# Score products with a pair of heads per row group, one q and one k transfer per tile, and an opening schedule that counts transfers in flight

## The chip, the cores and the metric

The kernel runs on one core of a Trainium2 chip. Its engines are TensorE (PE in the profile; its weight loads are PEld), VectorE (DVE), ScalarE (ACT), GpSimd (POOL) and SyncE (SP), which here only issues transfers. The metric is the device time of one execution in microseconds (us). Three runs of the kernel before gave 946.87, 948.35 and 951.93 us, a median of 948.35 us.

## The reference

Banded attention over 8 batches of 576 positions with 8 heads of 64 features, then a feed-forward layer with a per-channel PReLU. q, k, v and alpha are float32, w_in and w_out float64; the result is float32.

```python
scores = scale * np.matmul(q, k.transpose(0, 1, 3, 2))          # scale = 1/8
mask = (rel >= 0) & (rel < 64)                                  # rel = query - key
scores = np.where(mask, scores, -1000000000.0)
attn = np.exp(scores - np.max(scores, axis=-1, keepdims=True))
attn = attn / (np.sum(attn, axis=-1, keepdims=True) + 1e-09)
x = np.matmul(attn, v)               # then heads side by side: (4608, 512)
h = x @ w_in                         # (512, 2048)
g = np.maximum(h, 0.0) + alpha * np.minimum(h, 0.0)
out = g @ w_out                      # (2048, 512)
```

Each weight is read as two 32-bit words, which the kernel joins into one float32 value.

## The kernel before, in words

The 4608 rows are 36 tiles of 128 rows. A query block of 64 rows sees its own 64 keys and the 64 before, so a tile needs three key blocks of 64. The 13 blocks of the feed-forward layer hold 2 tiles three times, then 3 tiles ten times (`SIZES`). A block passes through 16 cells; cell f is one slice of 128 of the 2048 hidden channels.

**Attention of a tile.** Products of queries and keys (`a_score`, L434 in the profile), masked maximum (`a_least`, L445, DVE), exponential with sum (`a_exp`, L452, ACT), reciprocal (L468), scaling (`a_scale`, L474, POOL), transposition (L491 on PE and a copy, in the opening; L486 on DVE later), product with v (`a_value`, L508), and a split of the result in a high and a low part `xh` and `xl`. A score bank of PSUM holds one of the tile's two query blocks u: its 128 partitions are two heads h of 64 queries, its four column groups the pairs e of heads. The k tile in SBUF has the features of query block u on partitions 64u to 64u+63, with the two key blocks that u sees; the middle key block of a tile stands there twice. It comes in two transfers of 256 KB, and q in four of 64 KB, each of 64 partitions by four runs of 64 numbers.

**Weights.** Each of the 32 half-cells c (even: a slice of w_in, odd: of w_out) is loaded in 512 KB (`fetch`, L327) and converted: bit operations and joins on DVE and ACT, a product (`pr`, L369, POOL), a high part (`hi`, ACT), a low part (`lo`, L384, POOL).

**A cell of a block.** `h` (12 matmuls, L566), slopes on ACT, maximum on DVE, high part `gh` on ACT, low part `gl` on POOL (L595), and per tile three matmuls into the output bank (`o`, L609).

**What sets the order.** Up to the end of block 2 (the opening) the order of all engines is written by `list_schedule`: `opening_graph` gives each step an engine, a duration, its predecessors and the buffers it takes; the step with the highest rank (longest way to the end plus `favour`, a table of numbers) among those ready goes first. Engines then run their steps strictly in that order. From block 3 on, `eighth` and `cell` interleave attention and feed-forward by hand. Transfers are issued from the queue of SP and, for the first two q tiles and alpha, from that of ACT. Eight completion semaphores (DMAHW0 to DMAHW7 in the listings below) are used in turn by all transfers; an issue that takes one still in use by an earlier transfer waits on the issuing engine until that transfer has landed, and everything behind it on this engine waits too. The graph before does not know of these eight lanes.

Of the kernel before, what the change touches and what calls it, by code (L numbers as in the profile page):

```python
# [9 lines left out]
F32 = mybir.dt.float32  # L10
# [26 lines left out]
def opening_graph():  # L37
# [3 lines left out]
    ops = {}  # L41

    def op(name, engine, busy, after=(), take=None, free=(), done=None):
        lag = {"PE": 0.25, "DVE": 0.12, "ACT": 0.13, "POOL": 0.10, "SP": 0.0, "DMA": 1.8}[engine]
        ops[name] = Op(engine, busy, busy + lag if done is None else done, list(after), take, list(free))

    def load(name, service, after=(), take=None, queue="SP"):
        op("i." + name, queue, 0.64, after, take)
        op(name, "DMA", service, ["i." + name])
# [6 lines left out]
    for t in range(EARLY + 1):  # L56
        queue = "ACT" if t < 2 else "SP"
        for u in range(2):
            load(f"k.{t}.{u}", 0.93, [f"s.{t-2}.{x}" for x in range(2)] if t > 1 else [])
            for h in range(2):  # L60
                load(f"q.{t}.{u}.{h}", 0.36, [f"s.{t-2}.{x}" for x in range(2)] if t > 1 else [], queue=queue)
        for u in range(2):
            load(f"v.{t}.{u}", 0.93, [f"av.{t-2}"] if t > 1 else [])
    for c in range(2 * NCELL):
        load(f"raw.{c}", 1.6 if c % 2 else 1.86, take=(f"raw.{c}", ["raw"]))

    for t in attention:
        bank = ["po", "psa"] if t < 2 else ["psa"]
        for u in range(2):
            op(f"s.{t}.{u}", "PE", 0.47, [f"k.{t}.{u}", f"q.{t}.{u}.0", f"q.{t}.{u}.1"]  # L70
               + ([f"s.{t-1}.0", f"s.{t-1}.1"] if t else []) + ([f"av.{t-2}"] if t > 1 else []),
               take=(f"s.{t}.{u}", bank))
# [37 lines left out]
    for n in range(3):  # L110
        pair = [2 * n, 2 * n + 1]
        for f in range(NCELL):
# [9 lines left out]
            for i, t in enumerate(pair):  # L122
                op(f"o.{t}.{f}", "PE", 0.69,
                   [f"gl.{n}.{f}", f"lo.{2*f+1}"] + ([f"o.{t}.{f-1}"] if f else []) + ([f"o.{t-1}.{f}"] if i else []),
                   take=(f"po.{t}", ["psa"] if t == 3 else ["po"]) if f == 0 else None,
                   free=[f"gh.{n}.{f}", f"gl.{n}.{f}"] if i else [])
                if f == last:
                    op(f"ev.{t}", "ACT", 0.55, [f"o.{t}.{f}"], take=(f"ev.{t}", ["raw"]), free=[f"po.{t}"])
                    op(f"i.out.{t}", "SP", 0.64, [f"ev.{t}"])
                    op(f"out.{t}", "DMA", 0.9, [f"i.out.{t}"], free=[f"ev.{t}"])  # L130
# [3 lines left out]
def list_schedule(ops, slots, favour):  # L134
# [24 lines left out]
    while True:  # L159
        for e in ENGINES:  # L160
# [3 lines left out]
            while ready[e]:  # L164
                key = heappop(ready[e])
                n = key[1]
                o, pool = ops[n], None
                if o.take:
                    pool = next((p for p in o.take[1] if left[p]), None)
                    if pool is None:  # L170
                        passed.append(key)
                        continue
                    left[pool] -= 1
                    held[o.take[0]] = pool
                begun[n] = now
                until[e] = now + o.busy
                order.append((n, pool))
# [28 lines left out]
TILE_FAVOUR = [122, 108, 421, -187, -579, -728, -394, -893, 447, -524, -457]  # L206
BLOCK_FAVOUR = [302, 419, -88, 274]
KIND_FAVOUR = dict(
    ad=(75, -133), alpha=(-234, -17), at=(4, 157), av=(-70, 137), ep=(27, 227), ev=(-23, 183),
    ex=(-140, -142), gh=(2, -54), gl=(-152, 142), h=(-163, 317), hi=(-27, -163), k=(-159, 26), la=(95, 31),  # L210
    le=(-217, -229), lo=(-272, -1), mn=(239, -62), mx=(-15, -67), o=(-107, 129), out=(35, -75),
    pr=(34, -352), q=(-94, -45), raw=(-50, 165), rc=(41, 37), s=(-114, 50), sc=(10, 126), sl=(225, 83),
    sm=(126, 51), td=(-235, -80), tu=(-331, 105), tw=(-163, 57), tx=(16, 33), v=(-199, 68), vl=(150, -51),
    xh=(-191, -103), xl=(-89, -85),
# [20 lines left out]
def banded_attention_then_prelu_ffn(  # L235
# [42 lines left out]
    masks = const.tile([P, 2, KW], F32, name="masks")  # L278
    nc.gpsimd.memset(masks, 0.0)

    for h in range(2):
        half = masks[h * W:(h + 1) * W]
        nc.gpsimd.affine_select(out=half, in_=half, compare_op=ALU.is_ge, fill=NEG,
                                base=W, pattern=[[0, 2], [-1, KW]], channel_multiplier=1)
        nc.gpsimd.affine_select(out=half, in_=half, compare_op=ALU.is_gt, fill=NEG,
                                base=0, pattern=[[0, 2], [1, KW]], channel_multiplier=-1)

    nc.gpsimd.memset(masks[:, 1, 0:W], NEG)
# [110 lines left out]
    def k_load(t, u):  # L399
        r = slice(u * D, (u + 1) * D)  # L400
        nc.sync.dma_start(of_tile(t, "k", [P, NP, 2, 2, W])[r].rearrange("d e b h w -> d e (b h w)"),
                          kT[:, :, 2 * t + u:2 * t + u + 2].rearrange("e d b h w -> d e (b h w)"))
# [10 lines left out]
    def load(t):  # L413
        for u in range(2):
            k_load(t, u)
            q_load(t, u, 0)
            q_load(t, u, 1)

# [3 lines left out]
    def a_score(t, halves=(0, 1), from_="psa"):  # L422


        d = st[t]
        q, k = d["q"], d["k"]
        s = d.setdefault("s", {})
        for u in halves:
            s[u] = a_bank(f"s_{t}_{u}", from_)
        for e in range(NP):  # L430
# [93 lines left out]
    def eighth(s):  # L524
# [3 lines left out]
        if k == 0:  # L528
            if t + 1 < NT:
                load(t + 1)  # L530
# [225 lines left out]
```

## Time and profile before

| | us |
|---|---|
| median of 3 runs | 948.35 |
| profiled execution | 949.72 |
| its span, first to last instruction | 948.0 |
| PE busy in the span | 920.7 |
| PE idle from 212 us on, ended by any wait | none |

The profiled execution lies 1.37 us above the median, and 1.7 us of it lie outside the span. PE is busy 97% of the span; DVE, ACT and POOL are busy 46%, 45% and 37%. Idle time of PE is printed with what ended it; the time of an engine that is not waited for costs nothing. A row of the timeline reads: start, duration, engine, line, operation, output<-inputs, shape, count, and in brackets the idle time before it with its releaser. A row of the windows reads: stretch, its length, busy time and count of PE, PEld, DVE, ACT and POOL, the granted TensorE clock, the busy share of the 16 DMA engines, and GB/s.

### The profile page before, as it was taken

The page shows a single profiled execution, that of the slowest core. Times are in us where ns is not written, and L with a number is a line of the kernel's source. Part 1 is how long each engine was busy: PE and PEld are TensorE (multiplying, and loading weights), DVE is VectorE, ACT ScalarE, POOL GpSimd, SP SyncE. Part 2 cuts the span into 40 slices and gives each one's busy share as a digit, 9 for nine tenths or more (in the row PEclk, how much of TensorE's full clock was granted, in tenths as well). Part 3 has the DMA queues.
Part 4 walks back from the last instruction along what each step waited for, and adds up shares of the span by engine and source line. Part 5 has one row for each costly group of instructions (what it writes and reads, how often), then busy time and mean ns, then how long its engine had stood idle before and what let it go on. Part 6 is the DMA issues. An engine that isn't in the chain of part 4 may idle for free.

```text
span 948.0 us, 17231 instructions
## 1 busy us (share of the span) xinstructions
PE 920.7 (97%) x6601; PEld 820.3 (87%) x6601; DVE 437.8 (46%) x1329; ACT 429.6 (45%) x1204; POOL 348.0 (37%) x329
## 2 busy tenths in 40 slices
PE   3989999999999999999999999999999999999998
PEld 2878788888888899888988888888988888898997
DVE  4778885213644444444444443443443444443111
ACT  3777777345434334434434344443443443432322
POOL 3679897232323322322332222233222223322221
PEclk9989999999999999999999999999999999999999
DMA  9997553123233323323323323223323332100000
GB/s 220 215 208 186 165 164 102 44 47 79 57 59 87 57 56 90 57 56 89 57 56 90 56 57 90 57 56 57 89 56 57 87 59 56 57 1 1 34 1 34
DMA packets 94385, 74.52 MB, mean 79 GB/s; under 512 B 42576, under 2 KB 87648, under 8 KB 94304
## 3 DMA queue, kind: packets, MB, share of 16 engines
q1 hardware_dynamic: 92096, 72.90, 35.0%
q8 instruction: 52, 0.85, 0.4%
q10 hardware_dynamic: 2208, 0.53, 0.4%
q14 instruction: 29, 0.24, 0.1%
HBM read 63.97 MB, written 9.44 MB: 77 GB/s over the span
## 4 chain that ended last, share of the span: by engine, by line
PE 87%; DMA 5%; POOL 2%; DVE 2%; issue 1%; ACT 1%; ACTq 0%; SPq 0%; DVEq 0%; POOLq 0%
PE h L566 40%; PE o L609 39%; PE s L434 4%; PE av L508 4%; DMA raw<-w_in 2%; DMA k<-kT 1%; DMA v<-vN 1%; POOL gl L595 1%; DMA q<-qT 1%; POOL val L369 1%; DMA raw<-w_out 1%; DVE two L336 0%; PE t L491 0%; POOL wout_l L384 0%; DVE man L346 0%
## 5 line engine op out<-in xcount | busy, mean ns | idle before, releaser
L595 POOL TENSOR_TENSOR gl<-g,gh 128x384 fp32r<-128x384 f32 (+1 forms) x208 | 197.1, 947 | 556.8 <-ACT gh L588 551.3
L581 DVE SCALAR_TENSOR_TENSOR g<-h,s_sb,g 128x384 f32<-128x384 f32 (+1 forms) x208 | 121.8, 586 | 337.1 <-ACT g L575 336.4
L575 ACT ACTIVATE g<-h,sa_sb 128x384 f32<-128x384 f32 (+1 forms) x208 | 115.5, 556 | 264.4 <-PE h L566 261.5
L609 PE MATMUL o<-wout_h,gl 128*128 128x512 f32 x576 | 228.5, 397 | 1.1 <-POOL gl L595 0.9
L609 PE MATMUL o<-wout_l,gh 128*128 128x512 f32 x576 | 227.3, 395 | 0.0
L609 PE MATMUL o<-wout_h,gh 128*128 128x512 f32 x576 | 224.7, 390 | 0.0
L566 PE MATMUL h<-xh,win_h 128*128 128x384 f32 (+1 forms) x832 | 175.2, 333 | 2.3 <-DVE g L581 2.3
L566 PE MATMUL h<-xl,win_h 128*128 128x384 f32 (+1 forms) x832 | 170.0, 326 | 0.0
L566 PE MATMUL h<-xh,win_l 128*128 128x384 f32 (+1 forms) x832 | 169.1, 325 | 0.0
L566 PEld LDWEIGHTS h<-xh,win_h 128*128 128x128 f32 x832 | 142.4, 190 | 21.5 <-DVE g L581 4.2
L588 ACT CAST gh<-g 128x384 fp32r<-128x384 f32 (+1 forms) x208 | 101.6, 489 | 129.2 <-DVE g L581 117.7
L486 DVE STREAM_TRANSPOSE pt<-w 32x256 f32<-32x256 f32 x324 | 141.2, 436 | 5.5
L566 PEld LDWEIGHTS h<-xl,win_h 128*128 128x128 f32 x832 | 143.6, 190 | 0.1
L566 PEld LDWEIGHTS h<-xh,win_l 128*128 128x128 f32 x832 | 140.9, 190 | 0.0
L609 PEld LDWEIGHTS o<-wout_h,gh 128*128 128x128 f32 x576 | 108.4, 188 | 24.3
L609 PEld LDWEIGHTS o<-wout_h,gl 128*128 128x128 f32 x576 | 108.5, 188 | 18.8 <-POOL gl L595 2.6
L452 ACT ACTIVATE w<-w,nm 128x128 f32<-128x128 f32 x288 | 113.1, 396 | 21.0 <-DVE nm L445 20.9
L609 PEld LDWEIGHTS o<-wout_l,gh 128*128 128x128 f32 x576 | 108.7, 189 | 13.5
L474 POOL TENSOR_TENSOR w<-w,rc 128x1024 f32<-128x1024 f32 (+1 forms) x45 | 70.0, 1555 | 15.6 <-DVE rc L468 15.5
L445 DVE CUSTOM_DVE_ANT_0 w<-s,masks 128x128 f32<-128x128 f32 x288 | 70.8, 283 | 4.9 <-PE s L434 4.5
L520 DVE TENSOR_TENSOR xl<-av,xh 128x512 fp32r<-128x512 f32 x36 | 24.8, 690 | 103.0 <-ACT xh L515 103.0
L434 PE MATMUL s<-k,q 64*64 64x128 f32 x1152 | 53.8, 292 | 15.3 <-DMA q<-qT 11.9
(46 smaller groups left out, 527.7 us busy)
## 6 DMA issues: line engine op xcount, KB each, us to landing
k<-kT SPq DMA_DIRECT2D x72, 256.0 KB, 5.0
v<-vN SPq DMA_DIRECT2D x72, 256.0 KB, 4.3
out<-os SPq DMA_DIRECT2D x36, 256.0 KB, 2.3
q<-qT SPq DMA_DIRECT2D x136, 64.0 KB, 4.7
raw<-w_in SPq DMA_DIRECT2D x16, 512.0 KB, 4.8
raw<-w_out SPq DMA_DIRECT2D x16, 512.0 KB, 6.2
q<-qT ACTq DMA_DIRECT2D x8, 64.0 KB, 6.2
alpha_rows<-alpha ACTq DMA_DIRECT2D x1, 8.0 KB, 4.0
```

What stands on the lines that cost most here:

```text
L434: nc.tensor.matmul(s[u][out_, e], q[r, e, h, :], k[r, e, :, h, :], start=True, stop=True)
L445: nc.vector.tensor_tensor_reduce(out=d["w"][:, g, :], in0=d["s"][u][:, e], in1=mask, op0=ALU.add, op1=ALU.min, scale=-SCALE, scalar=3.0e38 ...
L452: nc.scalar.activation(w, w, AF.Exp, scale=-1.0, bias=d["nm"][:, g:g + 1], accum_out=d["sm"][:, g:g + 1])
L474: nc.gpsimd.tensor_tensor(out=w, in0=w, in1=rc.unsqueeze(2).broadcast_to(list(w.shape)), op=ALU.mult)
L486: nc.vector.transpose(pt[ks, :, r], w[r, :, ks])
L508: nc.tensor.matmul(av[r, e, u * W:(u + 1) * W], v[:, e, u, r], pt[:, u * NP + e, h * W:(h + 1) * W], start=True, stop=True)
L566: nc.tensor.matmul(ph[:, :nt], wt[:, c, fs], xt[:, c, xs], start=(k == 0), stop=(k == 3 * NP - 1))
L575: nc.scalar.activation(g, ph[:, :nt], AF.Copy, scale=sa_sb[:, f:f + 1])
L581: nc.vector.scalar_tensor_tensor(out=g, in0=ph[:, :nt], scalar=s_sb[:, f:f + 1], in1=g, op0=ALU.mult, op1=ALU.max)
L588: nc.scalar.copy(gh, gs[n, f])
L595: nc.gpsimd.tensor_tensor(out=gl, in0=g, in1=gh.bitcast(F32), op=ALU.subtract)
L609: nc.tensor.matmul(po[t], gt[:, ts], wt[:, f, :], start=(f == 0 and k == 0), stop=(f == NF - 1 and k == 2))
```

## The change

**Layout of the scores.** A row group of 64 partitions now holds one head x of a pair instead of one query block. A score bank holds head x of each pair; its partitions are the two query blocks u, its columns the pairs (a, h). So q and k need only one copy of each number: k is 128 partitions by two runs of 384 numbers (three key blocks, 384 KB), q 128 partitions by two runs of 256 numbers (256 KB), one transfer each. Masks get a third variant, and `a_value` reads its weights under the new index. Counts and shapes of the matmuls, of the DVE and of the ACT steps stay as they are.

**Order of the score products.** In tiles 0 to 2 (`WHOLE`) the products of both banks are one step of the opening, alternating between the row groups; in tiles 3 to 8 of the opening each bank is still a step of its own. From block 3 on both banks alternate, as before.

**The schedule.** `lane=8` is a buffer that every transfer takes at its issue and frees when it lands. Durations in the graph are changed (loads, scores), and both tables of `favour` hold other numbers.

```diff
+WHOLE = (0, 1, 2)
-SLOTS = dict(ph=2, psa=3, po=3, raw=3, exp=2, val=2, g=2, gh=3, gl=3)
+SLOTS = dict(ph=2, psa=3, po=3, raw=3, exp=2, val=2, g=2, gh=3, gl=3, lane=8)
...
+    def load(name, service, after=(), take=(), queue="SP"):
+        op("i." + name, queue, 0.64, after, [take] * bool(take) + [("lane " + name, ["lane"])])
+        op(name, "DMA", service, ["i." + name], free=["lane " + name])
...
-        queue = "ACT" if t < 2 else "SP"
+        done = [f"s.{t-2}.0", f"s.{t-2}.1"] if t > 1 else []
+        load(f"q.{t}", 1.05, done, queue="ACT" if t == 0 else "SP")
+        load(f"k.{t}", 1.6, done)
...
-        load(f"raw.{c}", 1.6 if c % 2 else 1.86, take=(f"raw.{c}", ["raw"]))
+        load(f"raw.{c}", 2.0 if c % 2 else 2.2, take=(f"raw.{c}", ["raw"]))
...
+        if t in WHOLE:
+            op(f"s.{t}.0", "PE", 0.94, score, take=[(f"s.{t}.0", bank), (f"s.{t}.1", bank)])
+            op(f"s.{t}.1", "PE", 0.0, [f"s.{t}.0"], done=0.0)
...
-TILE_FAVOUR = [122, 108, 421, -187, -579, -728, -394, -893, 447, -524, -457]
+TILE_FAVOUR = [305, -52, 78, 372, -192, -315, -70, -391, 34, -311, -259]
...
-    def k_load(t, u):
-        r = slice(u * D, (u + 1) * D)
-        nc.sync.dma_start(of_tile(t, "k", [P, NP, 2, 2, W])[r].rearrange("d e b h w -> d e (b h w)"),
-                          kT[:, :, 2 * t + u:2 * t + u + 2].rearrange("e d b h w -> d e (b h w)"))
-
-    def q_load(t, u, h, queue=None):
-        r = slice(u * D, (u + 1) * D)
-        (queue or nc.sync).dma_start(of_tile(t, "q", [P, NP, 2, W])[r, :, h, :],
-                                     qT[:, :, t, h, u * W:(u + 1) * W].rearrange("e d q -> d e q"))
+    def q_load(t, queue=None):
+        (queue or nc.sync).dma_start(of_tile(t, "q", [P, 2, 2 * P]),
+                                     qT[:, :, t].rearrange("(a x) d h p -> (x d) a (h p)", x=2))
+
+    def k_load(t):
+        nc.sync.dma_start(of_tile(t, "k", [P, 2, 6 * W]),
+                          kT[:, :, 2 * t:2 * t + 3].rearrange("(a x) d b h w -> (x d) a (b h w)", x=2))
...
-        for e in range(NP):
+        for x, from_ in zip(halves, banks):
+            s[x] = a_bank(f"s_{t}_{x}", from_)
+        for a in range(2):
             for h in range(2):
-                for u in halves:
-                    r, out_ = slice(u * D, (u + 1) * D), slice(h * W, (h + 1) * W)
-                    nc.tensor.matmul(s[u][out_, e], q[r, e, h, :], k[r, e, :, h, :],
-                                     start=True, stop=True)
+                for u in range(2):
+                    for x in halves:
+                        r, us = slice(x * D, (x + 1) * D), slice(u * W, (u + 1) * W)
+                        nc.tensor.matmul(s[x][us, 2 * a + h], q[r, a, h, us], k[r, a, u:u + 2, h, :],
+                                         start=True, stop=True)
```

Three places show how the order moves. First, the transfers at the start, each with the semaphores its issue waits for: SP before (raw is a half-cell of weights).

```order
L327 DMA raw_117<-w_in 128x4x256
L327 DMA raw_120<-w_out 128x1024
L327 DMA raw_123<-w_in 128x4x256
L401 DMA k_126<-kT 64x4x256 [waits DMAHW1_49]
L401 DMA k_126<-kT 64x4x256 [waits DMAHW4_49]
L401 DMA k_132<-kT 64x4x256 [waits DMAHW6_49]
L401 DMA k_132<-kT 64x4x256 [waits DMAHW7_49]
L410 DMA v_139<-vN 64x4x256 [waits DMAHW0_49]
```

And SP now:

```order
L410 DMA k_118<-kT 128x2x384
L414 DMA v_121<-vN 64x4x256 x2
L406 DMA q_124<-qT 128x2x256
L410 DMA k_126<-kT 128x2x384
L333 DMA raw_128<-w_in 128x4x256
L333 DMA raw_130<-w_out 128x1024 [waits DMAHW0_49]
L333 DMA raw_150<-w_in 128x4x256 [waits DMAHW1_49]
L414 DMA v_152<-vN 64x4x256 [waits DMAHW2_49]
L406 DMA q_167<-qT 128x2x256 [waits DMAHW3_49,PE_49]
L410 DMA k_169<-kT 128x2x384 [waits DMAHW4_49]
```

The three weight loads stood ahead of the first k and now stand behind q and k of two tiles. ACT's queue before held eight q transfers of 64 KB and alpha, of which four waited for a lane; it now holds q of tile 0 and alpha, and neither waits.

Second, PE up to the first cell `h_0`. Before (s_0 and s_1 of one tile are its banks, t its transpositions):

```order
L434 MATMUL s_0_165<-k_126,q_115 64x128 x8
L434 MATMUL s_1_185<-k_126,q_115 64x128 x8
L434 MATMUL s_0_208<-k_132,q_128 64x128 x8
L491 MATMUL t_0_240<-ident,w_177 128x128 x4
...
L491 MATMUL t_0_315<-ident,w_221 128x128 x4
L434 MATMUL s_0_340<-k_235,q_200 64x128 x8
L434 MATMUL s_1_356<-k_235,q_200 64x128 x8
L491 MATMUL t_1_369<-ident,w_221 128x128 x4
L508 MATMUL av_396<-pt_110,v_146 64x64 x16
L434 MATMUL s_0_424<-k_307,q_260 64x128 x8
L491 MATMUL t_0_438<-ident,w_351 128x128 x4
L566 MATMUL h_0_449<-xh,win_h 128x256 x4
```

Now (in tiles 0 to 2 the rows of s_0 and s_1 alternate eight times):

```order
L433 MATMUL s_0_132<-k_118,q_116 64x128
L433 MATMUL s_1_133<-k_118,q_116 64x128
...
L651 MATMUL alpha_t<-ident,alpha_rows 128x16
L433 MATMUL s_0_186<-k_126,q_124 64x128
...
L490 MATMUL t_0_282<-ident,w_208 128x128 x4
L433 MATMUL s_0_306<-k_169,q_167 64x128
...
L490 MATMUL t_1_357<-ident,w_208 128x128 x4
L507 MATMUL av_371<-pt_111,v_152 64x64 x16
L433 MATMUL s_0_392<-k_227,q_213 64x128 x8
L433 MATMUL s_1_408<-k_227,q_213 64x128 x8
L565 MATMUL h_0_432<-xh,win_h 128x256 x4
```

Both banks of tile 3 now stand ahead of `h_0`, and the first transposition of tile 2 behind it.

Third, POOL around the second scaling of tile 1 (w_221 before, w_208 now), on which the transposition t_1 of that tile waits. Before:

```order
L474 TENSOR_TENSOR w_221<-w_221,rc_224 128x512
L369 TENSOR_TENSOR val_304<-val_304,exp_163 128x512
L369 TENSOR_TENSOR val_313<-val_313,exp_197 128x512
L474 TENSOR_TENSOR w_221<-w_221,rc_224 128x512
L384 TENSOR_TENSOR wout_l<-val_304,wout_h 128x512
```

Now:

```order
L473 TENSOR_TENSOR w_208<-w_208,rc_211 128x512
L375 TENSOR_TENSOR val_292<-val_292,exp_280 128x512
L375 TENSOR_TENSOR val_301<-val_301,exp_294 128x512
L390 TENSOR_TENSOR win_l<-val_292,win_h 128x4x128
L473 TENSOR_TENSOR w_208<-w_208,rc_211 128x512
```

The first half-cell's low part is now made between the two scalings; before, half-cell 0 was done ahead of both.

More of the change, by code (lines that the diff above doesn't have):

```diff
@@ L41, in opening_graph, with op @@
     ops = {}
-    def op(name, engine, busy, after=(), take=None, free=(), done=None):
+    def op(name, engine, busy, after=(), take=(), free=(), done=None):
         lag = {"PE": 0.25, "DVE": 0.12, "ACT": 0.13, "POOL": 0.10, "SP": 0.0, "DMA": 1.8}[engine]
[L45 to L49, printed above, removed]
+        ops[name] = Op(engine, busy, busy + lag if done is None else done, list(after), [take] if take and isinstance(take[0], str) else list(take), list(free))
+    def load(name, service, after=(), take=(), queue="SP"):
+        op("i." + name, queue, 0.64, after, [take] * bool(take) + [("lane " + name, ["lane"])])
+        op(name, "DMA", service, ["i." + name], free=["lane " + name])
     attention = range(EARLY)
@@ L128, in opening_graph @@
                     op(f"ev.{t}", "ACT", 0.55, [f"o.{t}.{f}"], take=(f"ev.{t}", ["raw"]), free=[f"po.{t}"])
-                    op(f"i.out.{t}", "SP", 0.64, [f"ev.{t}"])
-                    op(f"out.{t}", "DMA", 0.9, [f"i.out.{t}"], free=[f"ev.{t}"])
+                    load(f"out.{t}", 0.9, [f"ev.{t}"])
+                    ops[f"out.{t}"].free.append(f"ev.{t}")
     return ops
@@ L166, in list_schedule @@
                 n = key[1]
[L167 to L174, printed above, removed]
+                o, got = ops[n], []
+                for key_, pools in o.take:
+                    p = next((p for p in pools if left[p] > got.count(p)), None)
+                    got.append(p)
+                if None in got:
+                    passed.append(key)
+                    continue
+                for (key_, _), p in zip(o.take, got):
+                    left[p] -= 1
+                    held[key_] = p
                 begun[n] = now
                 until[e] = now + o.busy
-                order.append((n, pool))
+                order.append((n, got))
                 heappush(ends, (now + o.busy, 0, n))
@@ new lines, in scores @@
+    def scores(t, u, banks):
+        if t not in WHOLE:
+            a_score(t, (u,), banks)
+        elif u == 0:
+            a_score(t, (0, 1), banks)
+    steps = {
+        "at": lambda got: alpha_turned(), "ad": lambda got: signs(),
+        "i.alpha": lambda got: nc.scalar.dma_start(alpha_rows, alpha.rearrange("(f p) -> f p", p=P)),
+        "i.k": lambda got, t: k_load(t), "i.q": lambda got, t: q_load(t, nc.scalar if t == 0 else None),
+        "i.v": lambda got, t, u: v_load(t, u),
+        "i.raw": lambda got, c: fetch(c),
+        "i.out": lambda got, t: m_store(t),
+        "s": lambda got, t, u: scores(t, u, got),
+        "le": lambda got, t, g: a_least(t, g),
+        "ex": lambda got, t, g: a_exp(t, g),
+        "sm": lambda got, t, u: a_sum(t, (u,)),
+        "rc": lambda got, t, u: a_inverse(t, (u,)),
+        "sc": lambda got, t, u: a_scale(t, (u,)),
+        "tu": lambda got, t, u: a_turn(t, u, got[0]),
+        "td": lambda got, t, u: a_turned(t, u),
+        "av": lambda got, t: a_value(t, got[0]),
+        "xh": lambda got, t: a_xh(t), "xl": lambda got, t: a_xl(t),
+        "tw": lambda got, c: mask_exponent(c), "tx": lambda got, c: exponent(c),
+        "mn": lambda got, c: mask_mantissa(c), "mx": lambda got, c: signed_mantissa(c),
+        "ep": lambda got, c: sign(c), "vl": lambda got, c: join(c),
+        "pr": lambda got, c: product(c), "hi": lambda got, c: high_part(c),
+        "lo": lambda got, c: low_part(c),
+        "h": lambda got, n, f: m_hidden(n, f), "sl": lambda got, n, f: m_slopes(n, f),
+        "la": lambda got, n, f: m_larger(n, f), "gh": lambda got, n, f: m_high(n, f),
+        "gl": lambda got, n, f: m_low(n, f),
+        "o": lambda got, t, f: m_add(t // 2, f, t % 2), "ev": lambda got, t: m_evict(t),
```

90 lines of the change are left out of this document (28 added, 62 removed).

## The prediction

> **What bounds the kernel now.** I read the page first, then what PE waited for, then windows over the span.
>
> ```profile
> PE 920.7 (97%) x6601; PEld 820.3 (87%) x6601; DVE 437.8 (46%) x1329; ACT 429.6 (45%) x1204; POOL 348.0 (37%) x329
> PE   3989999999999999999999999999999999999998
> ```
>
> PE is busy almost throughout; the holes are in the first slices. The waits of PE up to 212 us:
>
> ```profile
> PE s L434 <- DMA q<-qT: 11.9, 1, 11.9
> PE t L491 <- POOL w L474: 3.2, 1, 3.2
> PE s L434 <- DMA k<-kT: 2.9, 2, 2.4
> PE h L566 <- DVE g L581: 2.3, 2, 2.0
> PE av L508 <- DVE pt L496: 1.2, 2, 0.8
> PE o L609 <- POOL gl L595: 0.9, 1, 0.9
> PE s L434 <- DVE val L363: 0.6, 1, 0.6
> ```
>
> They add up to 23.0 us of idle time; behind 212 us the same view has no row. So the 736 us from block 3 on are PE work back to back, and what an engine or a transfer gains there is hidden. The change keeps the matmuls there: same counts, same shapes, and banks alternating between row groups before and after. It can move the time only through the opening, and what PE loses or gains there goes to the end one for one.
>
> ```profile
> 2.00:12.00 10.00, 0.12 (x2) 0.16 (x4) 1.98 (x3) 1.55 (x2) 1.35 (x5) 1.00 1.11 248
> 12.00:67.00 55.00, 46.29 (x433) 39.11 (x434) 40.83 (x148) 38.97 (x131) 34.54 (x31) 0.95 1.08 216
> 67.00:160.00 93.00, 90.53 (x648) 78.33 (x648) 73.62 (x168) 69.52 (x175) 84.14 (x80) 0.98 0.60 158
> 212.00:948.00 736.00, 731.81 (x5100) 657.04 (x5099) 310.04 (x971) 296.28 (x838) 211.88 (x187) 1.00 0.27 58
> ```
>
> Three stages in the opening. To 67 us the DMA engines are full (share 1.08) at 216 GB/s; the other engines wait in turns. From 67 to 160 us POOL is the busiest beside PE (84 of 93 us, mostly weights). Then PE alone. In the first stage PE also runs at half rate for long:
>
> ```profile
> 11.88 1.97 PE L434 MATMUL s<-k,q 64*64 64x128 f32 x16 [11.88 <-DMA q<-qT]
> 14.34 2.90 PE L434 MATMUL s<-k,q 64*64 64x128 f32 x32 [0.49 <-DMA k<-kT]
> 20.40 1.12 PE L491 MATMUL t<-ident,w 128*128 128x128 f32 x4 [3.16 <-POOL w L474]
> 25.46 1.76 PE L508 MATMUL av<-pt,v 128*64 128x64 f32 x28 [0.37 <-DVE pt L496]
> 28.20 2.89 PE L434 MATMUL s<-k,q 64*64 64x128 f32 x32
> 33.36 1.76 PE L508 MATMUL av<-pt,v 128*64 128x64 f32 x28 [0.81 <-DVE pt L496]
> 37.72 1.20 PE L566 MATMUL h<-xh,win_h 128*128 128x256 f32 x4
> 40.43 0.63 PE L491 MATMUL t<-ident,w 128*128 128x128 f32 x4
> 61.64 1.97 PE L434 MATMUL s<-k,q 64*64 64x128 f32 x16 [0.57 <-DVE val L363]
> 228.51 1.10 PE L434 MATMUL s<-k,q 64*64 64x128 f32 x32
> ```
>
> Four transpositions take 1.12 us at 20.40 and 0.63 at 40.43: up to about 40 us the clock is half, although the profile's clock column still prints 1.00 there. It falls twice more, where the column shows it:
>
> ```profile
> 60.00:70.00 10.00, 9.43 (x64) 8.45 (x65) 7.58 (x26) 6.60 (x21) 7.04 (x8) 0.66 1.06 221
> 110.00:120.00 10.00, 7.95 (x40) 6.85 (x40) 7.18 (x13) 5.93 (x12) 7.52 (x9) 0.83 0.47 159
> ```
>
> At 0.66 and 0.83 of full speed for 10 us, 3.4 and 1.7 us are lost, each behind a gap of 2 to 3 us.
>
> The Trainium skill, "TensorE: Matmul & The Clock Gate", part 1 on the HAM clock gate, says that the clock halves after an idle window of about 3.4 us and opens after about as much sustained work. The trace disagrees both ways: a gap of 2.0 us was followed by half rate, and the 7.1 us without a gap from 33.36 to 40.43 were needed to open it. By the rule, short gaps would cost themselves only, and the last term below would have 5.1 us less to win; as no place of the trace bears it out, it gets no chance of its own.
>
> **The change, part by part.**
>
> *The first wait, -6.3 us.* Before, three weight loads stand ahead of k, and ACT stands in its own queue until a lane is free.
>
> ```profile
> 0.80 0.44 SPq L327 DMA_DIRECT2D raw<-w_in  x1
> 5.12 6.49 SPq L401 DMA_DIRECT2D k<-kT  x4
> 5.13 0.69 DVE L346 TENSOR_SCALAR man<-raw 128x512 int32<-128x512 int32 x1 [4.14 <-DMA raw<-w_in]
> 10.44 1.28 ACT L341 ACT_TABLE_LOAD   x1 [10.44 <-DMA q<-qT]
> 4.00:6.00 2.00, 0.00 (x0) 0.00 (x0) 0.87 (x2) 0.00 (x0) 0.00 (x0) 1.00 1.05 314
> ```
>
> The first weight load, 524 KB at the head of SP's queue beside q on ACT's, was usable at 5.13. Now q (262 KB) heads one queue and k (393 KB) the other. 655 KB at 248 to 314 GB/s, from about 2 us on, are there at 4.1 to 4.6, and half a microsecond for completion and overlap with v behind k gives about 5.1; I take 5.6. Bounds: 4.8, and 8.3 if all 1.8 MB issued first come at once. PE starts at 5.6 instead of 11.88.
>
> *Score products, -2.4 us of work ahead of the first cell.* In the table above, 16 matmuls of one bank cost 1.97 us at half rate, and 32 alternating ones 1.10 at full rate, so about 2.2 at half rate (no row shows it). Tiles 0 to 2 cost 1.97 + 2.90 + 1.97 + 2.89 = 9.7 before (32 of them from 14.34 take 2.90) and 3 x 2.2 = 6.6 now: -3.1. Against it, bank 1 of tile 3 moves ahead of the first cell (+0.9, from 1.97 to 2.89) and a transposition behind it (-1.1), which come back later with the other sign; with small remainders of the alpha and value steps I take -2.4. Bounds: 0, if a whole tile at half rate costs 2.9 and the gaps absorb it, and -4.
>
> *Gaps ahead of the first cell, +4.7 us.* Before, they are 0.49, 3.16, 0.37 and 0.81, together 4.8. Now by the order listed: tile 1's q and k are the last of 1.84 MB, at 270 GB/s (between the windows' 248 and 314) at about 9.3; the scores of tile 0 end at 7.8, so 1.5. Then t_0 of tile 0: before, the first maximum ran at 16.00 and the transposition at 20.40, 4.4 us later; now the first maximum is at 7.9, and the alpha steps (0.8 us of DVE) stand between: 13.1 against an end of tile 1's scores at 11.5, so 1.6. Small ones 0.3. Tile 2's k ends 4.3 MB, at 270 GB/s about 18.5, no gap. The large one is t_1 of tile 1. It waits for the second scaling on POOL, now queued behind two products and a low part, and in PE's order the scores of tiles 2 and 3 don't both stand ahead of it.
>
> ```profile
> 16.00 0.28 DVE L445 CUSTOM_DVE_ANT_0 w<-s,masks 128x128 f32<-128x128 f32 x1
> 26.35 2.51 POOL L369 TENSOR_TENSOR val<-val,exp 128x512 f32<-128x512 f32 x2 [0.52 <-DVE val L363]
> 28.82 1.03 POOL L474 TENSOR_TENSOR w<-w,rc 128x512 f32<-128x512 f32 x1
> 31.05 1.27 POOL L384 TENSOR_TENSOR win_l<-val,win_h 128x512 fp32r<-128x512 f32 x1
> 13.62 0.68 DVE L363 SCALAR_TENSOR_TENSOR val<-raw,man 128x512 f32<-128x512 uint32 x1
> ```
>
> DVE's steps of that stretch at 0.6 each put the first product's input at about 21.5 and the second's at 23.3; then 1.28 (POOL), 1.27 and 1.03 end the scaling at 26.9, t_1 at 27.0, where PE has been free since 21.8: 5.2. A copy before the values of tile 1 adds 0.9. Sum 9.5, so +4.7. Bounds: 0 (DVE's estimate is 5 us late) and +9.
>
> The three terms put the first cell at about 33.7 instead of 37.72: -4.0.
>
> *The rest of the opening, -4.0 us.* Before, PE loses 0.9, 2.4, 0.6, 2.3 in gaps and 3.4 and 1.7 in clock behind 38 us: 11.3. What was late there was data:
>
> ```profile
> 30.21 8.82 DMA k<-kT
> 39.05 8.60 DMA v<-vN
> 47.71 10.02 DMA raw<-w_in
> q1 hardware_dynamic: 2280, 3.39, 55.8%
> q1 hardware_dynamic: 36976, 24.91, 30.3%
> ```
>
> The chain of waits runs through three transfers from 30 to 57.7 us. What they cost comes from the two last rows, which are 80 to 100 us (mostly weights: 2280 packets and 3.39 MB in 55.8% of 16 engines for 20 us, 78 ns and 1487 bytes each) and 300 to 700 us (tiles: 36976 packets, 24.91 MB, 52 ns and 674 bytes). A straight line through both is an estimate of 31 ns a packet and 0.032 ns a byte. A tile's q, k and v before are 1024 packets of 256 bytes and 1024 of 1 KB: 105 us of one engine, 6.6 us of all 16. Now 256 and 512 of 1 KB and 256 of 1.5 KB: 69, or 4.3 us. About six tiles loaded from 12 to 67 us thus free some 13 us of DMA time. POOL and DVE get work earlier but have as much of it, 35 and 41 us from 12 to 67 us. In the order listed POOL also holds `gl` of the first cell ahead of four steps that are ready, some 4 us. So I take a third of the 11.3 us. Bounds: -11.3, and +6 if a new gap of 2.4 us with 3.4 us of clock is added.
>
> The Trainium skill, "DMA: Bandwidth & Descriptors", rules for kernel authors, asks for one transfer of 128 partitions instead of two of 64, since both share the same engines. By that, the halves cost no more than one transfer and only the repeated key block (131 KB of 1.31 MB a tile) would be saved, 0.6 us a tile at 216 GB/s; the rest of this term would have to come from the packets.
>
> *Later.* A tile's 2.2 us of DMA time less, its four issues less on SP and the third mask are worth nothing behind 212 us: DMA share is 0.27 there and no wait of PE ends. If that cover were gone the transfers would gain 36 x 2.2 us at most, but PE's back-to-back work doesn't allow it.
>
> Sum: -6.3 - 2.4 + 4.7 - 4.0 = -8.0. The profiled execution, 949.72 (span 948.0 and 1.7 outside), would become 941.7. It stands 1.37 above the median, so against the median I forecast 940.3.
>
> **The rivals.**
>
> *The lead is given back (944 to 950).* PE starts 6 us earlier, but the weights come later: the first weight load was usable at 5.13 and is now the sixth transfer, at about 11. If POOL's queue of conversions sets PE's pace at 45 to 60 us (by the steps above, the low part of half-cell 4 ends at about 47.5 against 45.65 + 1.31 before), the lead becomes a gap at h or o of the first cells, and only the shorter score work and about 1 us are left: about -3, 945.5. For it: POOL's stretch from 67 us is 90% busy. Against: in the same time PE can work on tile 3 and block 1, which the order has earlier.
>
> *Slower (953 to 958).* The mechanism is the clock behind POOL's gap. If t_1 of tile 1 waits beyond 30 us (POOL's products wait for ACT, which is behind tile 1's exponentials), the first cell is no earlier than before, and tile 3, h and o then come in short bursts with gaps of over 2 us, each paying 2.4 us and 3.4 of clock as at 60 us. From two such gaps more than before it decides: +11.6, less the 6.3 of the start, +5.3, about 953.5.
>
> *All of it (930 to 934).* The DMA time freed carries through: no gap at 60 and 115 us, both drops of the clock gone. Then the last term is -11.3 and the sum -15.3: 933. For it, the chain of waits; against, POOL's 84 of 93 us.
>
> *The transfers are no cheaper.* If a packet costs by its bytes, DMA saves 10% of a tile; the start is won all the same, the last term falls to about -1: 943.5, inside the forecast's range.
>
> **How the numbers follow.** The forecast (-5 to -12) has 0.55, with the cheap-transfer case in it; the lead given back 0.22; slower 0.09; all of it 0.14. A measurement of this kernel tells 0.5%, 4.7 us, from no change. Faster by more: the forecast and all of it, 0.69, less 0.02 for its edge, 0.67. Within 0.5%: 0.23. Slower: 0.10. The likeliest case alone reaches from 936 to 943.5; the range that leaves out some 2 in 10 goes from 931.5 to 947.5.
>
> **What would show it.** The first score matmul at 5 to 6.5 us; scores of tile 0 in about 2.2 us; a gap of some 5 us at PE's t, released by POOL, between 20 and 28 us; the first h at 32 to 35 us; DMA below full share before 67 us, by a tile's cheaper loads; no wait of PE for k or q later than 20 us; nothing changed from block 3 on (some 736 us). A first h later than 37 us, or more than two waits over 2 us of PE between 40 and 120 us, would make the forecast wrong; so would any change of the length of the late stage.

## The result, and the profile after

The changed kernel takes 934.48 us (median of 4 runs, 934.10 to 934.98), the kernel before 950.14 (4 runs, 946.87 to 952.83). The ratio is 0.9837, with a 95% interval of 0.9801 to 0.9873: 1.6% faster. The profiled execution took 934.54, with a span of 932.8 us against 948.0, so 15.2 us less. The forecast was 940.3; what came is nearest to the case listed as "all of it" (930 to 934), 0.5 us above its upper edge.

Windows over the span of the changed kernel (columns as before):

```profile
2.00:12.00 10.00, 3.93 (x65) 3.49 (x65) 2.54 (x22) 4.22 (x17) 2.50 (x7) 1.00 1.07 289
12.00:67.00 55.00, 46.53 (x432) 37.97 (x426) 48.08 (x148) 44.55 (x139) 41.31 (x39) 1.00 0.81 223
67.00:160.00 93.00, 92.71 (x691) 81.60 (x690) 68.67 (x156) 68.38 (x167) 80.98 (x79) 1.00 0.47 146
197.00:932.80 735.80, 732.10 (x5102) 657.23 (x5100) 310.35 (x971) 296.55 (x839) 211.90 (x187) 1.00 0.19 53
```

The late stage is the same length, 735.8 us against 736.0, and begins 15 us earlier. From 12 to 67 us the DMA share fell from 1.08 to 0.81 while the bytes per second rose a little, and DVE and POOL were busier in the same stretch: 48.1 and 41.3 us against 40.8 and 34.5. What PE waited for up to 197 us:

```profile
PE s L433 <- DMA q<-qT: 6.1, 1, 6.1
PE t L490 <- POOL w L473: 3.4, 3, 1.6
PE s L433 <- DVE nm L444: 2.0, 1, 2.0
PE s L433 <- DVE val L369: 1.9, 2, 1.2
PE o L608 <- POOL gl L594: 1.2, 2, 1.0
PE t L490 <- DVE pt L495: 0.9, 1, 0.9
PE t L490 <- DVE val L369: 0.5, 1, 0.5
PE av L507 <- DVE pt L495: 0.3, 2, 0.2
PE h L565 <- DVE g L580: 0.3, 1, 0.3
```

Together 16.6 us, against 23.0. All but 0.6 of the 6.4 us are the first wait; the later ones are as long in sum (10.5 against 11.1) but shorter one by one. And the timeline of PE:

```profile
6.06 1.98 PE L433 MATMUL s<-k,q 64*64 64x128 f32 x32 [6.06 <-DMA q<-qT]
10.27 2.10 PE L433 MATMUL s<-k,q 64*64 64x128 f32 x32 [2.01 <-DVE nm L444]
21.43 0.69 PE L433 MATMUL s<-k,q 64*64 64x128 f32 x2 [0.72 <-DVE val L369]
23.28 1.98 PE L433 MATMUL s<-k,q 64*64 64x128 f32 x30 [1.16 <-DVE val L369]
26.86 1.12 PE L490 MATMUL t<-ident,w 128*128 128x128 f32 x4 [1.61 <-POOL w L473]
32.86 0.74 PE L565 MATMUL h<-xh,win_h 128*128 128x256 f32 x4
38.11 0.50 PE L608 MATMUL o<-wout_h,gl 128*128 128x512 f32 x1 [1.02 <-POOL gl L594]
```

The first `h` runs at full rate (0.74 us for four; 1.20 before), so the clock opens at about 32.6 instead of 40.4, and the clock column prints 1.00 from there to the end of the opening: neither drop of before comes back. An account of the 15.2 us, which is an estimate in that half rate counts as half of the busy time under it: before, 23.8 us of work up to 40.4 cost 11.9, and the two drops 5.1, together 17.0; now 18.0 us of work up to 32.6 cost 9.0. That is 8.0 us from the clock, 5.8 from the first wait (11.88 to 6.06), 0.6 from the later waits, and the remainder, about 1, goes to the shorter score work by subtraction alone.

### The profile page after: what moved, and what is told of

The parts are those of the page before. It is cut to its first block, busy times and chain, and to the rows that moved or that the text cites. A ratio compares the mean times of both kernels' runs of the same rounds, so it can differ in the third digit from the quotient of the medians.

```text
span 932.8 us, 17053 instructions
## 1 busy us (share of the span) xinstructions
PE 912.3 (98%) x6601; PEld 812.3 (87%) x6601; DVE 438.0 (47%) x1329; ACT 430.5 (46%) x1204; POOL 348.1 (37%) x330
## 4 chain that ended last, share of the span: by engine, by line
PE 94%; DVE 2%; POOL 2%; ACT 1%; DMA 1%; issue 0%; POOLq 0%; DVEq 0%
PE h L565 43%; PE o L608 42%; PE s L433 4%; PE av L507 4%; PE t L490 1%; ACT w L451 1%; POOL val L375 1%; DMA q<-qT 1%; POOL w L473 0%; POOL gl L594 0%; POOL wout_l L390 0%; POOL win_l L390 0%; DVE exp L363 0%; DVE val L369 0%; DVE two L342 0%
## 5 line engine op out<-in xcount | busy, mean ns | idle before, releaser
L433 PEld LDWEIGHTS s<-k,q 64*64 64x64 f32 x1152 | 39.4, 142 | 24.0 <-PE o L608 9.6
```

What stands on the lines that cost most here:

```text
L433: nc.tensor.matmul(s[x][us, 2 * a + h], q[r, a, h, us], k[r, a, u:u + 2, h, :], start=True, stop=True)
```

## The experiments

Each but the last was timed beside the kernel before, whose medians there were 947.9 to 948.7. Differences below are against the changed kernel's 934.5 or against the neighbour named.

**New layout and transfers, order of before.**

```diff
-        "i.k": lambda pool, t, u: k_load(t, u),
-        "i.q": lambda pool, t, u, h: q_load(t, u, h, nc.scalar if t < 2 else None),
+        "i.k": lambda pool, t, u: k_load(t) if u == 0 else None,
+        "i.q": lambda pool, t, u, h: q_load(t, nc.scalar if t < 2 else None) if u + h == 0 else None,
...
-        "s": lambda pool, t, u: a_score(t, (u,), pool),
+        "s": lambda pool, t, u: a_score(t, (u,), (pool,)),
```

This is the kernel before with `k_load`, `q_load`, `a_score`, `a_value` and the masks of the change; its graph, slots and tables stay. k and q of a tile go out whole at the place of their first part.

> The kernel before, with the new layout of q, k and scores and its single transfers of q and k per tile, but the opening written in the order of before: old graph, no lanes, old tables, scores bank by bank, three weight loads first. Theory A (the transfers' DMA time is what the opening won): the DMA-bound stretch up to 67 us shortens, the gap at 60 us and both drops of the clock go, the first score still waits for the weight loads (9 to 11 us); 938 to 942, so two thirds or more of the 15 us. Theory B (the planned order is what won): the order of before stalls at other places as it did, 945 to 950.

Measured: 934.53 (933.10 to 936.03), ratio 0.9862 (0.9839 to 0.9886). Theory A said 938 to 942 and theory B 945 to 950; both are too high, B is out. The order of before, fed by the new transfers, is as fast as the newly planned one. Its waits, windows and timeline:

```profile
PE s L428 <- DMA k<-kT: 10.3, 1, 10.3
PE t L485 <- POOL w L468: 2.7, 2, 2.3
PE av L502 <- DVE pt L490: 1.8, 2, 1.6
```

```profile
12.00:67.00 55.00, 48.96 (x502) 41.87 (x497) 46.38 (x170) 47.31 (x162) 43.29 (x41) 0.97 0.81 230
```

```profile
10.27 3.81 PE L428 MATMUL s<-k,q 64*64 64x128 f32 x48 [10.27 <-DMA k<-kT]
31.00 1.20 PE L560 MATMUL h<-xh,win_h 128*128 128x256 f32 x4
```

It starts PE 4 us later than the changed kernel, since its weight loads go first, and still has the first `h` 2 us earlier. Its conversions begin earlier: DVE's first step on a weight comes at 5.5 us, and at 14.5 in the changed kernel. The DMA share is the same 0.81. The clock column reads 0.97 because of one piece of 3.4 us at half rate from about 30.4 on, which the second row above shows (1.20 us for four `h`). It follows a wait of 1.62 us:

```profile
28.52 0.92 PE L502 MATMUL av<-pt,v 128*64 128x64 f32 x24 [1.62 <-DVE pt L490]
```

This kernel has the new layout, the new transfers and the freed queue of ACT together. So it shows that the gain does not need the new plan, and not yet which part of the transfers brings it.

**q in runs of 256 bytes, one transfer.**

```diff
-        (queue or nc.sync).dma_start(of_tile(t, "q", [P, 2, 2 * P]),
-                                     qT[:, :, t].rearrange("(a x) d h p -> (x d) a (h p)", x=2))
+        (queue or nc.sync).dma_start(of_tile(t, "q", [P, 2, 2 * P]).rearrange("p a (g w) -> p (a g) w", g=4),
+                                     qT[:, :, :, :, t].rearrange("a g x d w -> (x d) (a g) w"))
```

> The changed kernel with one thing undone: q lies in memory so that one transfer of 256 KB consists of 1024 runs of 256 bytes instead of 256 runs of 1 KB. Same order, same number of transfers, same bytes. Theory A (price by packets, 31 ns each from the two rows in the prediction): 768 packets more are 24 us of one engine, 1.5 us of all 16 per tile, DMA near full up to 50 us again; 936 to 940, with the first score 0.5 to 1 us later. Rival (price by bytes): 934 to 935 and a first score at 6.1.

Measured: 934.29 (933.57 to 935.68), first score at 5.8. No time is lost, as the rival said, though the packets have a price. The DMA groups from 300 to 700 us give the price of the runs, first this kernel, then the changed one:

```profile
q1 hardware_dynamic: 32451, 23.28, 24.1%
```

```profile
q1 hardware_dynamic: 19764, 23.09, 21.0%
```

12687 packets more for nearly the same bytes take 3.1% of 16 engines for 400 us, 198 us: 16 ns each, half of the 31 that I worked out. DMA share from 12 to 67 us rises from 0.81 to 0.87, still below full, and behind the first two tiles' scores no wait of PE ends with a transfer.

**q and k in two transfers of 64 partitions.**

```diff
-        nc.sync.dma_start(d, kT[:, :, 2*t:2*t+3].rearrange("(a x) d b h w -> (x d) a (b h w)", x=2))
+        for x in range(2):
+            nc.sync.dma_start(d[x * D:(x + 1) * D], kT[x::2, :, 2*t:2*t+3].rearrange("a d b h w -> d a (b h w)"))
```

q is split in the same way.

> The changed kernel with q and k of a tile each in two transfers of 64 partitions instead of one of 128: same packets, same bytes, same order, two issues more per tile and lanes used up faster than the plan counts. If the number of transfers matters (issue time, 0.4 to 0.6 us each on SP, and lanes): waits of SP for lanes in the first 60 us and 936 to 939. If only packets and bytes matter: 934 to 935.

Measured: 937.38 (936.92 to 938.90), ratio 0.9895 (0.9875 to 0.9915): 2.9 us more. The packets of a tile are the same (this window holds 0.9 MB more), yet the share from 300 to 700 us rises:

```profile
q1 hardware_dynamic: 21200, 23.99, 24.8%
```

```profile
12.00:67.00 55.00, 46.01 (x439) 37.64 (x432) 45.80 (x144) 43.71 (x139) 39.38 (x37) 0.88 0.95 225
```

From 21.0% with 23.09 MB to 24.8% with 23.99 MB; the bytes alone would be 21.8. So halves cost DMA time of their own, about as much for each MB as the short runs of q did (1.03% for each MB in both runs, 0.91% in the changed kernel), and from 12 to 67 us the engines are near full again. Whether the 2.9 us come from that or from the additional issues is not separated: up to 70 us, SP's waits that end with a transfer add up to 4.0 us here and to 1.7 in the changed kernel. The Trainium skill, "DMA: Bandwidth & Descriptors", rules for kernel authors, says that two halves share the same engines and that one transfer of 128 partitions is to be used. The advice holds here; the reading that halves cost no more than the whole, on which the prediction weighed it, does not.

**Scores of tiles 0 to 2 bank by bank.**

```diff
-            a_score(t, (0, 1), banks)
+            a_score(t, (0,), banks[:1])
+            a_score(t, (1,), banks[1:])
```

> The changed kernel with the score products of tiles 0 to 2 written bank after bank, in the same places of PE's order, instead of alternating between the row groups. If they set the pace: 32 of them take 2.9 instead of 2.0 us at half rate, two of the three on the chain that ends last, so the first h 1.5 to 2.5 us later and 936 to 937. Rival: they end in the gaps in front of t, 934.5.

Measured: 935.94 (934.74 to 936.72), 1.5 us above the changed kernel, at the edge of what the runs tell apart. Tile 0's scores take 2.89 us instead of 1.98 and the first `h` comes at 33.82 instead of 32.86, which supports the first reading with about half its size for `h`. Tile 1 also shows what its scores wait for; the view of the changed kernel names DVE (`nm`), and here it is k:

```profile
10.13 2.89 PE L433 MATMUL s<-k,q 64*64 64x128 f32 x32 [0.79 <-DMA k<-kT]
```

**Lanes not counted in the plan.**

```diff
-SLOTS = dict(ph=2, psa=3, po=3, raw=3, exp=2, val=2, g=2, gh=3, gl=3, lane=8)
+SLOTS = dict(ph=2, psa=3, po=3, raw=3, exp=2, val=2, g=2, gh=3, gl=3, lane=99)
```

> The changed kernel, with 99 lanes in the planner's graph, so that it plans as if any number of transfers could be in flight; tables and everything else as in the change. If counting the lanes matters, the order has issues that wait on SP for a lane with others behind them, and the time is 937 to 942. Rival: with so few transfers eight lanes hardly bind, 934 to 936.

Measured: 934.80 (934.22 to 935.57). The rival holds: with one transfer each for q and k, counting lanes is worth nothing.

**Tables of before in the new plan.**

```diff
-TILE_FAVOUR = [305, -52, 78, 372, -192, -315, -70, -391, 34, -311, -259]
-BLOCK_FAVOUR = [539, 231, 26, -322]
+TILE_FAVOUR = [122, 108, 421, -187, -579, -728, -394, -893, 447, -524, -457]
+BLOCK_FAVOUR = [302, 419, -88, 274]
...
```

> The changed kernel with the two tables of rank corrections of the kernel before; layout, transfers, lanes and durations in the graph as in the change. If the tables carry the gain: 943 to 950. If the transfers carry it: 935 to 939, with gaps of PE of 3 us or more than the change has.

Measured: 940.00 (939.24 to 942.29), between the two expectations. Its longest waits (alpha's transposition stands first in this order, so its 6.1 us are the start):

```profile
PE t L490 <- POOL w L473: 6.3, 3, 3.4
PE alpha_t L651 <- DMA alpha_rows<-alpha: 6.1, 1, 6.1
PE s L433 <- DMA k<-kT: 4.7, 1, 4.7
```

The old tables fit the old graph (934.5 above) and not the new one, on which the new tables are 5.5 us better. Neither pair of graph and tables wins over the other.

**Three weight loads first.**

```diff
+        for c in range(3):
+            fetch(c)
         for name, got in list_schedule(graph, SLOTS, favour)[0]:
...
-        "i.raw": lambda got, c: fetch(c),
+        "i.raw": lambda got, c: fetch(c) if c > 2 else None,
```

> The changed kernel with the first three weight loads issued ahead of k of tile 0, as before the change, the rest of the order kept. If the first wait passes on one for one: first score at 9 to 11 us, the first h at 36 to 38, 938 to 940. Rival: the conversions that now stand in DVE's order behind tile 1 start no earlier, but the tile chain has slack in the DMA stage, so that part of it is made up by 60 us: 935 to 937.

Measured: 939.15 (938.96 to 940.21).

```profile
10.22 1.99 PE L433 MATMUL s<-k,q 64*64 64x128 f32 x32 [10.22 <-DMA k<-kT]
36.95 1.22 PE L565 MATMUL h<-xh,win_h 128*128 128x256 f32 x4
```

The first score is 4.2 us later, the first `h` 4.1, the time 4.7. In the planned order of the change the first wait passes on one for one. That the order of before starts at 10.27 without this loss shows that it is a property of the order: there the weights' steps stand in front and use the time (from 2 to 12 us DVE is busy for 5.6 us there and for none here).

**ACT free in the kernel before.**

```diff
-        "i.q": lambda pool, t, u, h: q_load(t, u, h, nc.scalar if t < 2 else None),
+        "i.q": lambda pool, t, u, h: q_load(t, u, h, nc.scalar if t < 1 else None),
```

> The kernel before with one edit: the four q transfers of tile 1 are issued from SP instead of ACT, so that ACT's queue holds only tile 0's q and alpha and waits for no lane. All transfers stay as small and as many. The order of before with the new transfers gave 934.5, and 6.7 of its 13.7 us were won by the first h already. Theory C (ACT's block at the start costs those): ACT's first step at about 3.5 instead of 10.4, conversions 5 us earlier, first h at 33 to 35, 942 to 945. Rival (transfers early on are simply fewer bytes and packets): the lanes that ACT frees are waited for on SP instead, first h at 36 to 38, 946 to 949.

Measured: 948.07 (946.53 to 953.70), ratio 1.0001 (0.9980 to 1.0022). ACT's first step comes at 4.2 instead of 10.4 and the first `h` 2 us earlier, and nothing is left of it in the time. In the profiled execution DMA stays full (1.16 from 12 to 67 us), and the clock falls at 59 and 117 us.

```profile
4.22 1.28 ACT L341 ACT_TABLE_LOAD   x1 [4.22 <-issue]
35.74 1.20 PE L566 MATMUL h<-xh,win_h 128*128 128x256 f32 x4
12.00:67.00 55.00, 47.25 (x428) 39.86 (x425) 37.34 (x142) 36.57 (x126) 32.53 (x30) 0.93 1.16 208
```

(These rows are of an execution 5.6 us above the median; the first two are from its first 36 us.) The time is the rival's, and theory C falls as a cause by itself.

**Many transfers from tile 2 on, and many up to tile 1.** Both have the new layout in the order of before (934.53), with q in four transfers of 64 partitions and k in two halves for some of the tiles only. q is read in runs of 256 bytes for all tiles, which cost no time above. In the second, all eight early q transfers go out from ACT, which waits for lanes again.

```diff
+        if t < 2:
+            (queue or nc.sync).dma_start(d.rearrange("p a (g w) -> p (a g) w", g=4),
+                                         qT[:, :, :, :, t].rearrange("a g x d w -> (x d) (a g) w"))
+            return
+        for x in range(2):
+            for a in range(2):
+                nc.sync.dma_start(d[x * D:(x + 1) * D, a].rearrange("p (g w) -> p g w", g=4),
+                                  qT[a, :, x, :, t].rearrange("g d w -> d g w"))
```

These are the lines for q of the first; the second has `t >= 2` in the condition, and its four transfers go to ACT's queue.

> The new layout with the order of before (934.5 us), but from tile 2 on q in four transfers of 64 KB in 256-byte runs and k in two halves, as many and as small as before; tiles 0 and 1 keep one transfer each. First h at 31 to 32 in any case. Theory D (DMA time and lanes after the start cost the other 7 us): DMA share over 1 from 12 to 67 us, PE waits for k or weights between 45 and 70 us, 938 to 942. Rival (what is won at the start carries through): 934 to 936.

> The mirror image: new layout, order of before (934.5), but q of tiles 0 and 1 in four transfers of 64 KB each and k in two halves, all eight q issued from ACT, which again waits there for lanes; from tile 2 on one transfer each. The other split (many from tile 2 on) cost 4.6 us. If the two parts add up to what the many transfers cost, this one costs the rest of the 13.7 us less the k bytes: ACT's first step at about 10.4, first h at 35 to 37, 939 to 942. Rival (freed DMA time later makes up a late start): first h as late, but no wait of PE for data behind it, 935 to 937.

Measured: 939.12 (937.62 to 943.93) and 938.61 (937.16 to 940.01), so 4.6 and 4.1 us more; by the intervals of their ratios each is known to some 3 us. The first `h` of the two, and the first kernel's window and DMA group from 300 to 700 us:

```profile
31.62 0.72 PE L571 MATMUL h<-xh,win_h 128*128 128x256 f32 x4
```

```profile
35.70 1.20 PE L571 MATMUL h<-xh,win_h 128*128 128x256 f32 x4
```

```profile
12.00:67.00 55.00, 45.38 (x464) 38.44 (x461) 40.91 (x160) 41.88 (x146) 37.77 (x35) 0.94 1.06 218
q1 hardware_dynamic: 34800, 24.00, 24.7%
```

The first kernel starts as well as the one with whole transfers and loses behind it: DMA share 1.06 from 12 to 67 us, as theory D said, and a drop of the clock at 56 us. The second has ACT's first step at 10.47, but behind the first `h` no wait over 1.1 us; its waits are the rival's and its time lies between the two readings. The two parts make 8.7 of the 13.7 us between the order of before with old and with new transfers, with the uncertainty of both. The rest was not isolated.

The DMA group shows that the first kernel does not bring back the transfers of before. It has as many and as small ones and still takes 1.03% for each MB, no more than the short runs or the halves alone took, where the kernel before took 1.22%. At least two things are left out in both kernels: the key block that was loaded twice, 131 KB of each tile's 1.31 MB, and the place where q lands. Before, q's runs of 256 bytes landed 512 bytes apart in SBUF (`[r, :, h, :]`); here and in the run with short runs they are read apart and land side by side. No run undoes either.

**TensorE kept busy at the start.**

```diff
+    def warming(count):
+        for _ in range(count):
+            nc.tensor.matmul(wp, warm_r[:, :P], warm_r, start=True, stop=True)
...
+        warming(9)
         for name, got in list_schedule(graph, SLOTS, favour)[0]:
...
-        "at": lambda got: alpha_turned(),
+        "at": lambda got: (alpha_turned(), warming(8)),
```

> The changed kernel with nine dummy matmuls of 128x512 on TensorE from about 1.5 us, before the first scores, and eight behind alpha's transposition, into a bank that is free then; the rest of the order kept. They only hold TensorE busy. If its clock opens before 8 us and stays open (the waits up to the first h are 2.0 us at most, now filled, and 1.6): half rate, which costs some 9 us up to 32.6, ends early; the chain to the first h holds scores, transpositions and values at half rate for about 9 us of its length, so 3 to 5 us are won: 929.5 to 931.5. Rival: the small matmuls and the waits close the clock again, or the chain is on ACT, DVE and POOL: 933 to 935.

Measured: 933.45 (932.96 to 934.24), ratio 0.9845 (0.9817 to 0.9873), 1.0 us under the changed kernel, from another set of runs, so hardly told apart.

```profile
1.62 4.21 PE L673 MATMUL warmed<-xh 128*128 128x512 f32 x9 [1.62 <-DVE xh L668]
9.70 1.22 PE L433 MATMUL s<-k,q 64*64 64x128 f32 x32
13.62 0.99 PE L490 MATMUL t<-ident,w 128*128 128x128 f32 x4 [0.88 <-DVE pt L495]
13.70:34.20 20.50, 15.23 (x151) 12.36 (x152) 17.04 (x67) 15.03 (x52) 11.51 (x10) 0.50 0.97 254
```

The clock opens (tile 1's scores take 1.22 instead of 2.10) and is at half again from 13.7 to 34.2, although the waits before 13.7 were 1.2 and 0.9 us. The time is the rival's: the clock does not stay open, and the first `h` comes at 31.88, only 1.0 us earlier. PE is busy for 15.2 of those 20.5 us, with small matmuls. Which of the two, the size of the matmuls or the waits between them, closes the clock is not shown.

**Forced waits of TensorE.**

```diff
         m_larger(n, f)
+        if 4 <= n < 12 and f in (4, 11):
+            for _ in range(GAPS[(2 * n + (f > 4)) % 8]):
+                nc.vector.tensor_scalar_mul(dum, dum, 0.5)
+            nc.tensor.matmul(ph[:16, :16], dum[:16, :16], dum[:16, :16], start=True, stop=True)
```

> The changed kernel with 16 forced waits of TensorE in blocks 4 to 11, where it otherwise never waits: behind 12 h matmuls a tiny matmul into the same bank waits for ACT and DVE to have read it and for 0, 3, 6, 9, 12, 15, 18 or 24 small DVE steps of about 0.2 us, each number twice. Its extra steps change nothing in the output. The gaps should be 1.5 to 6.5 us, some 55 us in all. Theory from the trace before: gaps of 2 us or more are followed by half rate for 3 to 7 us. Theory by the rule of the page on the clock gate: only gaps of more than about 3.4 us are. With the first, the time is 55 us and 1.7 to 3.4 us for each of some 12 gaps more, 1010 to 1030; with the second for some 7, 1000 to 1015.

Measured: one execution, 1043.9 us, span 1042.2. The waits came out longer than planned, 75.2 us in all.

```profile
330.42 0.21 PE L649 MATMUL h<-ident 16*16 16x16 f32 x2 [3.60 <-DVE ident L648]
377.37 0.23 PE L649 MATMUL h<-ident 16*16 16x16 f32 x2 [5.17 <-DVE ident L648]
416.19 0.21 PE L649 MATMUL h<-ident 16*16 16x16 f32 x2 [2.04 <-DVE ident L648]
641.20 0.21 PE L649 MATMUL h<-ident 16*16 16x16 f32 x2 [1.39 <-DVE g L584]
```

```profile
332.00:335.40 3.40, 3.40 (x11) 3.03 (x11) 1.96 (x8) 0.88 (x4) 0.00 (x0) 0.50 0.00 0
376.40:383.20 6.80, 5.83 (x39) 4.47 (x43) 0.81 (x4) 0.00 (x0) 0.00 (x0) 0.50 0.00 0
417.30:420.70 3.40, 3.40 (x11) 2.85 (x10) 2.42 (x9) 0.88 (x4) 0.00 (x0) 0.51 0.02 5
641.00:650.00 9.00, 8.80 (x97) 7.50 (x98) 2.05 (x8) 2.24 (x5) 1.02 (x1) 1.00 0.24 64
```

All 14 waits of 2.04 us and more were followed or accompanied by half rate, for 3.4, 6.8 or once 10.2 us; the two of 1.4 us were not. The span is 109.4 us longer than the changed kernel's; without the waits that leaves 34 us, 2.4 for each of the 14. The first theory holds, for this one execution. The rule of the Trainium skill ("TensorE: Matmul & The Clock Gate", part 1), with an idle window of about 3.4 us, would have left the waits of 2.04 at full rate; the measurement decides against it here.

## Why the prediction was right, and where it was wrong

**The bound.** That only the opening counts was right: 735.8 against 736.0 us from block 3 on.

**The first wait.** Right: first score at 6.06 where 5.6 was taken, and one for one in this order by the run with the weights first. The order of before does without it (10.27 and the same time).

**Score products.** Right: tile 0 in 1.98 us where 2.2 was taken; bank by bank costs 1.5 us. The term itself was loosely added up: its named parts (-3.1, +0.9, -1.1) make -3.3, and -2.4 was taken for "small remainders". PE's work ahead of the first `h` fell from 21.0 to 18.3 us, -2.7.

**Gaps ahead of the first cell.** Right in sum, wrong in part: t_1 of tile 1 at 26.86 where 27.0 was forecast, and the scaling on POOL is its releaser. But the 5.2 us are not one gap: tile 2's scores wait 0.7 and 1.2 us for a PSUM bank that the mantissa of a weight holds until `val` (I had them run ahead), and 1.6 remain. So the sign "a gap of some 5 us at PE's t" did not come. The gap of 2.0 us ahead of tile 1's scores is k's, as forecast (1.5). The view names the first maximum on DVE, but that had ended at 8.51. k of tile 1 was issued at 3.37 and landed 6.8 us later, at 10.2, and with the scores bank by bank the same scores start at 10.13 with k as the releaser. The gaps ahead of the first `h`, without the first wait, are 8.5 us where 9.5 was taken; the first `h` came at 32.86, forecast 33.7.

**The rest of the opening.** This step failed in size: "a third of the 11.3 us", -4.0, where 10.3 came (15.2 less the 4.9 by which the first `h` is earlier). 9.3 of them are what the step lists: behind the first cells PE now waits 2.0 us instead of 6.2, and the clock's 5.1 are gone; the remaining 1 goes by subtraction to the first cell, which now runs at full rate. That data was late was right: with the new layout and its transfers the order of before wins the same 13.7 us. What held me back were POOL's busy time and `gl` in front of steps that are ready. POOL's load was no bound but a queue that had waited for data: as data came it did 41.3 us of work from 12 to 67 instead of 34.5. The `gl` cost one wait of 1.0 us.

**The price of a packet.** Wrong by parts, and near in sum by luck. 31 ns a packet measured 16 where q's runs alone are cut; halves cost extra, which I took as nothing. For a tile, 105 less 69 gave 36 us of one engine. From 300 to 700 us, by the bytes of a tile with its result (1.57 MB before, 1.44 now), a tile took 122 us of one engine before and takes 84 now, 38 less. But with transfers from tile 2 on as many and as small as before it takes 95, so many and small transfers explain 11 of the 38. The other 27 lie in what no run undoes, the key block loaded twice and q's landing among them. A line through two mixed rows gave no price of one part.

**The rivals.** "All of it" had 0.14, and its mechanism came: no gap at 60 and 115 us, both drops of the clock gone; 934.5 lies just outside its 930 to 934. That the forecast's range holds 934.5 too is owed to its width: the likeliest case alone began at 936. "The lead is given back" and "slower" did not come: the longest wait left behind the first cells is 1.0 us, and the clock stays. "The transfers are no cheaper" is out by the DMA shares.

**The clock.** The prediction read 7.1 us without a gap as needed to open it. That is not so: it opened 5.7 us after the last wait over 0.2 us here (26.86 to 32.6), and 4.5 and 5.8 us after the forced waits of 2.04 and 5.17 us ended. That a gap of 2.0 us is followed by half rate held.

**The change's own words.** The new plan, its lanes and its tables, which the forecast worked through queue by queue, brought nothing over the order of before (934.48 against 934.53), though in its own order most of its steps behaved as computed. I had not asked whether the old order with the new transfers would do as well.

## What to carry to other kernels

Before a new order is worked out, run the old order with the new transfers: where a saturated DMA stage sets the pace, they can be the entire gain. An engine that is 90% busy behind a full DMA stage is not thereby the next bound; look whether its idle time ended with data, and let it speed up with the data. When a view names a releaser that had ended long before, look for a transfer that landed just ahead. And in the midst of dense matmuls count a wait of TensorE of 2 us or more at its own length and some 2.4 us of clock, while the two waits of 1.4 us cost themselves alone. Among the small matmuls of an opening less is enough: 1.62 us in the order of before with the new transfers was followed by 3.4 us at half rate.

## What the runs showed of the hardware that was not expected

Two transfers of 64 partitions with the same packets took more DMA time than one of 128 (24.8 against 21.0% for 4% more bytes), about as much more for each MB as cutting q's runs from 1 KB to 256 bytes did (24.1% for 1% more bytes, and no time). The two together took no more than either (24.7% for 4% more bytes), so the prices of single causes do not add up here. A clock opened by dense dummy matmuls was at half rate again at 13.7 us, 4.1 us behind the last of them, under small matmuls with waits of about 1 us, though in the dense stage two waits of 1.4 us did not close it. How thin work must be for that was not tried.
